# Six blocks of distance, eight transposed tiles, a bias on VectorE and another table of durations in a planned attention and Fourier kernel

## The chip, the core and the metric

One core of a Trainium2 chip runs the whole program. The engines are PE (TensorE, matrix products; PEld is its loading of weights), DVE (VectorE), ACT (ScalarE), POOL (GpSimd) and SP (SyncE, which only issues transfers here). The metric is the device time of one execution in microseconds (us); the time of a kernel is the median of its runs.

## The reference

Two layers read inputs of their own, and their outputs stand side by side, 2048 rows of 1024 + 1024 numbers.

```python
# A: attention with a window, 32 heads of 32 numbers
qkv = x @ wqkv                                   # 2048 x 3072
scores = q k^T * 32 ** -0.5
mask = (i - j >= 0) & (i - j < 256)              # a query sees itself and the 255 keys before it
p = softmax(where(mask, scores, -1e9))
a = (p v, heads side by side) @ wo               # 2048 x 1024
# B: Fourier mixing
y = dft_seq_re @ (x @ dft_hid_re.T) - dft_seq_im @ (x @ dft_hid_im.T)
concat([a, y], axis=-1)
```

All is in fp32 in the reference. The kernel holds each fp32 matrix as a sum of two fp16 matrices (hi and lo) and builds each large product out of three fp16 passes, hi.hi, hi.lo and lo.hi. The large square products are also cut in quarters and made from seven products instead of eight.

## The kernel before

**Stages.** First come the projections to q, k and v, which go to buffers in memory (`qs`, `vs`). Then attention runs block by block, and while it runs PE also does the second half of the projections and nearly the whole Fourier layer (lines with `m` at L720, 512 columns each). Last comes the product with `wo`. So PE has two streams of work, attention and the large products, and a number `rate` says how many attention blocks are recorded for each large product.

**One block of attention** (`s_step`) is 128 queries of two heads. There are 256 blocks, ordered by half of the sequence (`pr`), group of four heads (`g`), chunk of 512 tokens (`sc`), pair of heads (`hp`) and tile of 128 tokens (`i`). PE writes the scores against the last two key tiles into one of two PSUM banks `s`, and those against the third key tile into the bank `old` (L586). DVE joins them by a predicated copy (L597) and takes the row maximum `mx` (L602). POOL turns the maximum into the bias of the exponential (L609, `bias`, two numbers a row). ACT makes two exponentials (L612) and the hi half `hl` of the probabilities (L432), DVE the lo half (L436); only then is the `s` bank free. SP issues a transposing transfer from `hl` to `t` (L621), and POOL masks it: a masked copy `z` for the third tile (L627), and `t` itself (L630).

**The value products** (`v_step`) take two blocks at once: 24 small matmuls or fewer each (L662) into the one bank `pv`, then three DVE operations (L667, L669, L673) that divide and write the tile `o`. They are recorded `LAG` blocks behind the scores. After eight blocks `o_step` splits `o` in two halves `ohl`, transposes them to `ot` and stores that.

**What sets the order.** Nothing is issued as it is recorded. `Plan.op` records each operation with an engine, an assumed duration, and what it reads and writes. `Plan.close` gives it a due time, counted back from the PE operations in the order of their recording with their assumed durations summed. `Plan.run` then plays the program once with the assumed durations; each engine that comes free takes the operation with the earliest due time among those whose inputs are there. The order so found is fixed in each engine's queue; on the chip each engine works its queue strictly in order. So an assumed duration has no direct effect on the chip: it changes who stands before whom.

**Buffers.** A `Ring` of n buffers makes the (k+n)-th user wait for the last use of the k-th. In attention: `qk1` holds a chunk of keys (three transfers, L417, since hi stands twice), `qk0` one of queries, `vt` one of values; `hl`, `t`, `z` and `o` are as above. In the second half of the sequence (`pr` 1) each head group loads three key tiles in turn: half of chunk 1, chunk 2, chunk 3.

Of the kernel before, what the change touches and what calls it, by code (L numbers as in the profile page):

```python
# [10 lines left out]
F32 = mybir.dt.float32  # L11
# [33 lines left out]
LAG = 4  # L45
# [3 lines left out]
TBUF = 6  # L49
# [251 lines left out]
def c_act(n, ap=True):  # L301
    return 0.19 + 0.00084 * n + (0.09 if ap else 0.0)
# [26 lines left out]
def c_mm(n):  # L329
    return max(0.032, n / 2400.0 + 0.0025)  # L330
# [3 lines left out]
def fused_kernel(ctx: ExitStack, tc: tile.TileContext, xa, wqk, wv, wo, xb, wd, cs, out):  # L334
# [111 lines left out]
    def dve(cost, fn, r=(), w=(), port=False):  # L446
        op("DVE", cost, fn, r=r, w=w, port=port)
# [20 lines left out]
    def scale_of(key, v, s, wk, down=2.0 ** -14, loose=False):  # L468
        t1 = tops.pop(key)
        pt = old_ring.new()  # L470
        op("PE", 0.26, lambda: nc.tensor.transpose(pt.t[:, :P], t1.t[:, 0:1].to_broadcast([P, P]), ident),
# [8 lines left out]
        dve(0.53, rest, w=[wk])  # L480
# [44 lines left out]
    z_ring = att_ring("z", [P, 4, P], F16, 4)  # L525
    rs_ring = att_ring("rs", [P, 2, 2], F32, 2)
    o_ring = att_ring("o", [P, QB * P], F32, 3)

    def attention():
# [33 lines left out]
        def s_step(b):  # L563
# [8 lines left out]
            def scores(dst, k0, k_end, w):  # L572
                mats, cost, keys = [], 0.0, []
                for j in range(2):
                    h, k = 2 * hp + j, k0
                    while k < k_end:
# [4 lines left out]
                        cost += c_mm((k1 - k) * P) + 0.01  # L581
# [23 lines left out]
            if BIAS == "ACT":  # L605
                op("ACT", 0.387, lambda: nc.scalar.activation(bias.t, mx.t, AF.Identity, bias=pshift, scale=es),
                   r=[mx, "pshift", ("esc", g // 2)], w=[bias])
            else:
                op("POOL", 0.215, lambda: nc.gpsimd.tensor_scalar(bias.t, mx.t, es, PSHIFT, op0=ALU.mult, op1=ALU.add),  # L609
                   r=[mx, ("esc", g // 2)], w=[bias], port=True)  # L610
# [23 lines left out]
        def v_step(b):  # L634
# [3 lines left out]
            if (g, sc) not in cur:  # L638
                cur[g, sc] = o_ring.new()
            for r in (1, 0):  # L640
# [6 lines left out]
                for j in range(2):  # L647
                    at = (2 * hp + j) * VW
                    for m, (part, kb) in enumerate(seq):
# [4 lines left out]
                        cost += 0.034  # L654
# [10 lines left out]
                op("PE", cost, run, r=list(dict.fromkeys(keys)), w=[pv])  # L665
# [10 lines left out]
                rs.t.unsqueeze(3).to_broadcast([P, 2, 2, DH]), op=ALU.mult), r=[pv, rs], w=[(o, hp, i)])  # L676

        def o_step(g, sc):
            o = cur.pop((g, sc))
            keys = [(o, hp, i) for hp in range(2) for i in (0, 2)]  # L680
            ohl, ot = o_ring.new(), o_ring.new()
            half = lambda h: (lambda: ohl.t.bitcast(F16).rearrange("p (h c) -> p h c", h=2)[:, h])
            split(half(0), half(1), lambda: o.t, None, 512, keys, [(ohl, 0)], [(ohl, 1)])
            op("SP", C_TURN, lambda: nc.sync.dma_start_transpose(
                ot.t.bitcast(F16).rearrange("p (a q) -> p a q", q=P), ohl.t.bitcast(F16)),
               r=[(ohl, 0), (ohl, 1)], w=[ot], dma=turned(8))
            op("SP", C_ISSUE, lambda: nc.sync.dma_start(ots[sc, :, g].rearrange("c h t -> c (h t)"), ot.t.bitcast(F16)),
# [1007 lines left out]
```

## Time and profile before

| what | value |
|---|---|
| median of 3 runs | 1731.82 us (1731.67 to 1733.55) |
| the profiled execution | 1732.34 us, span 1730.6 us |
| PE busy | 1690.7 us, 98% |
| DVE busy | 1346.4 us, 78% |
| ACT busy | 1056.7 us, 61% |
| POOL busy | 776.7 us, 45% |
| clock granted to TensorE | 1.00 |

The span runs from the first to the last instruction of the profile. A group of the profile is named by line, engine, operation and tiles (out<-in). Behind its busy time stands the time in which the engine was idle just before it, and who ended that. Matmuls overlap: one of 512 columns is listed at 379 ns, though they follow each other faster than that.

### The profile page before, as it was taken

Reading aid. Unit: us, or ns where it says so; the run is one execution under the profiler, and the core shown is the slowest. Engines: PE = TensorE matmul, PEld = TensorE weight load, DVE = VectorE, ACT = ScalarE, POOL = GpSimd, SP = SyncE. Lnnn points to the kernel's source line nnn. Section 1 sums busy time; section 2 is a strip of 40 time slices with the busy share of each in tenths; the row PEclk is TensorE's granted clock in tenths of the full one; section 3 lists DMA queues with packets and bytes.
Section 4 is the critical chain, followed back from the end, with each engine's and each line's share of the span. In section 5 each row is a group of like instructions: output and inputs, shape, how many; then the busy total and the mean of one; then the engine's idle time right before and its main releaser. Section 6 shows DMA issues by size and latency. Waiting matters only on the chain.

```text
span 1730.6 us, 31866 instructions
## 1 busy us (share of the span) xinstructions
PE 1690.7 (98%) x11607; PEld 907.7 (52%) x11607; DVE 1346.4 (78%) x2294; ACT 1056.7 (61%) x1678; POOL 776.7 (45%) x979
## 2 busy tenths in 40 slices
PE   8999999999999999999999999999999999999998
PEld 3446787674545445545445555545555555544443
DVE  6978997677987888777798986789886688879641
ACT  7555635456767778777685756676665676553322
POOL 0133501314545646535765755676564666611000
PEclk9999999999999999999999999999999999999999
DMA  6389799999999779898499999769999658983331
GB/s 261 124 321 334 233 306 263 279 227 240 230 258 235 145 192 233 205 271 202 96 220 279 254 266 215 145 141 237 245 258 231 151 128 204 221 269 110 110 98 73
DMA packets 469918, 368.36 MB, mean 213 GB/s; under 512 B 341760, under 2 KB 412416, under 8 KB 469760
## 3 DMA queue, kind: packets, MB, share of 16 engines
q1 hardware_dynamic: 468896, 363.17, 81.0%
q0 software_dynamic: 864, 3.15, 1.2%
q8 instruction: 91, 1.49, 0.4%
q14 instruction: 67, 0.55, 0.1%
HBM read 195.97 MB, written 96.86 MB: 169 GB/s over the span
## 4 chain that ended last, share of the span: by engine, by line
PE 54%; DVE 15%; issue 8%; DMA 7%; ACT 7%; POOL 7%; SPq 1%; POOLq 0%; DVEq 0%; ACTq 0%
PE m L720 48%; PE pv L662 3%; POOL raw L1075 2%; DVE mx L602 2%; DVE st L1102 2%; ACT s L612 2%; POOL bias L609 2%; PE s L586 2%; DVE hl L436 2%; DMA t<-hl 1%; DVE s L597 1%; POOL t L630 1%; POOL z L627 1%; ACT hl L432 1%; DMA qk<-qs 1%
## 5 line engine op out<-in xcount | busy, mean ns | idle before, releaser
L720 PE MATMUL m<-reg,st 128*128 128x512 f16 x4776 | 1093.6, 379 | 13.6 <-DVE st L1102 3.6
L720 PEld LDWEIGHTS <-st 128*128 128x128 f16 x5400 | 512.5, 97 | 583.8 <-issue 15.1
L612 ACT ACTIVATE s<-s,bias,escs 128x256 f32<-128x256 f32 (+1 forms) x512 | 271.1, 530 | 286.2 <-POOL bias L609 277.4
L609 POOL TENSOR_SCALAR bias<-mx,escs 128x2 f32<-128x2 f32 x256 | 120.9, 472 | 400.5 <-DVE mx L602 308.6
L1075 POOL TENSOR_TENSOR raw<-raw,raw 128x512 f32<-128x512 f32 x128 | 175.8, 1374 | 186.6 <-DVE st L1102 174.7
L436 DVE TENSOR_TENSOR hl<-s,hl 128x512 f16<-128x512 f32 (+1 forms) x256 | 171.1, 669 | 96.5 <-ACT hl L432 95.7
L627 POOL TENSOR_SCALAR_AFFINE_SELECT z<-t 128x512 f16<-128x512 f16 x224 | 170.9, 766 | 60.0 <-DMA t<-hl 43.6
L630 POOL TENSOR_SCALAR_AFFINE_SELECT t<-t 128x512 f16<-128x512 f16 x224 | 170.5, 767 | 10.9
L602 DVE TENSOR_REDUCE mx<-s 128x2 f32<-128x512 f32 (+1 forms) x256 | 170.9, 668 | 4.8
L432 ACT ACTIVATE hl<-s 128x512 f16<-128x512 f32 (+1 forms) x256 | 148.0, 579 | 6.5 <-DMA t<-hl 3.1
L720 PEld LDWEIGHTS <-reg 128*128 128x128 f16 x1212 | 115.7, 98 | 63.2 <-issue 1.8
L1102 DVE SCALAR_TENSOR_TENSOR st<-raw,sc,st 128x1024 f16<-128x1024 f32 x96 | 134.1, 1400 | 16.5 <-ACT st L1101 16.2
L586 PEld LDWEIGHTS <-qk 96*128 96x128 f16 x1056 | 94.1, 97 | 85.8 <-issue 17.3
L1101 ACT ACTIVATE st<-raw,sc 128x1024 f16<-128x1024 f32 x96 | 109.6, 1146 | 34.5 <-PE m L720 14.5
L597 DVE COPY_PREDICATED s<-upper,old 128x256 f32<-128x256 uint32 x224 | 94.4, 421 | 29.3 <-PE old L586 21.8
L720 PE MATMUL m<-reg 128*128 128x512 f16 x480 | 114.7, 379 | 0.8 <-DVE reg L1512 0.5
L586 PE MATMUL s<-qk,qk 96*128 96x128 f16 (+1 forms) x608 | 96.0, 252 | 5.0 <-DVE hl L436 4.8
L720 PE MATMUL m<-xz,st 128*128 128x512 f16 x432 | 97.0, 379 | 3.4 <-ACT m L1193 3.4
L662 PE MATMUL pv<-vt,t 128*128 128x65 f16 x1984 | 98.4, 185 | 1.1 <-POOL t L630 1.0
L1512 DVE SCALAR_TENSOR_TENSOR ybig<-m,fu,ybig 128x512 f32<-128x512 f32 x112 | 83.4, 745 | 14.1 <-PE m L720 12.1
L662 PEld LDWEIGHTS <-t 128*128 128x128 f16 x1984 | 88.2, 96 | 9.8 <-POOL t L630 1.5
L662 PE MATMUL pv<-vt,z 128*128 128x65 f16 (+1 forms) x896 | 87.9, 185 | 4.2 <-DVE o L673 4.0
(172 smaller groups left out, 2124.7 us busy)
## 6 DMA issues: line engine op xcount, KB each, us to landing
raw<-in_cs_dram SPq DMA_DIRECT2D x64, 512.0 KB, 5.6
qk<-qs SPq DMA_DIRECT2D x192, 128.0 KB, 4.2
out_dram<-ybig SPq DMA_DIRECT2D x44, 512.0 KB, 5.4
qs<-ybig SPq DMA_DIRECT2D x64, 256.0 KB, 4.6
raw<-in_xb_dram SPq DMA_DIRECT2D x32, 512.0 KB, 5.4
raw<-in_wd_dram SPq DMA_DIRECT2D x32, 512.0 KB, 5.4
ybig<-out_dram SPq DMA_DIRECT2D x32, 512.0 KB, 5.3
vs<-ybig SPq DMA_DIRECT2D x32, 260.0 KB, 4.4
```

The costliest lines, as they stand in the source:

```text
L432: else nc.scalar.activation(dst(), src(), AF.Copy), r=r, w=w)
L436: op("DVE", c_dve(n), lambda: nc.vector.tensor_tensor(dst(), src(), hi(), op=ALU.subtract), r=r, w=w, port=port)
L586: nc.tensor.matmul(dst(j, a, e), qu.t[:, h, i * P:i * P + P], ku.t[:, h, ka:ke], start=True, stop=True, skip_group_check=True)
L602: dve(c_dve(2 * w), lambda: nc.vector.tensor_reduce(mx.t, sv(), axis=AX.X, op=ALU.max, negate=True), r=[(S, 0), (S, 1)], w=[mx])
L609: op("POOL", 0.215, lambda: nc.gpsimd.tensor_scalar(bias.t, mx.t, es, PSHIFT, op0=ALU.mult, op1=ALU.add), r=[mx, ("esc", g // 2)], w=[bias ...
L612: op("ACT", 0.32 + 0.00085 * w, lambda h=h: nc.scalar.activation(sv()[:, h], sv()[:, h], AF.Exp, bias=bias.t[:, h:h + 1], scale=es), r=[bi ...
L627: op("POOL", 0.637, lambda: nc.gpsimd.affine_select(out=z.t, in_=pk(), compare_op=ALU.is_gt, fill=0.0, base=0, pattern=[[0, 4], [-1, P]], ...
L630: op("POOL", 0.637, lambda: nc.gpsimd.affine_select(out=pk(), in_=pk(), compare_op=ALU.is_ge, fill=0.0, base=0, pattern=[[0, 4], [1, P]], ...
L662: nc.tensor.matmul(pvt()[:, r, j, lo:], lhs, vt.t[:, k % QB, at + lo:at + VW], start=a, stop=e, skip_group_check=True)
L720: nc.tensor.matmul(ps.t[:, j * n:j * n + n], lhs(), rhs(), start=first, stop=last, skip_group_check=True)
L1075: lambda: e.tensor_tensor(o(), a(), b(), op=ALU.subtract if sub else ALU.add), r=r, w=w, port=True)
L1102: op("DVE", c_dve(n, True), lambda: nc.vector.scalar_tensor_tensor(dst(1), src(), scl(), dst(0), op0=ALU.mult, op1=ALU.subtract), r=[*r, s ...
```

## The change

- `LAG` goes from 4 to 6: value products are recorded six blocks behind the scores.
- The ring `t` goes from 6 to 8 tiles. To make room, `qk1` goes from 3 to 2, `vt` from 3 to 2, `z` from 4 to 3, `o` from 3 to 1. The output halves `ohl` and `ot` now come from the rings `hl` and `t`, which the blocks of probabilities use. A key "turn" makes the first value product of a chunk follow the last `o` of the chunk before it.
- The bias moves from POOL to DVE (256 operations), with the assumed duration `C_TINY` (0.155).
- Assumed durations: ACT operations of 512 elements 0.60 where it was 0.62 (0.68 where 0.71, with a scale); a value matmul 0.0265 or 0.0297 where it was 0.034; a score matmul 0.01 less; a PE transposition 0.12 where it was 0.26; the three small operations of a scale 0.47 where it was 0.53.

```diff
-LAG = 4
+LAG = 6
...
-TBUF = 6
+TBUF = 8
...
 def c_act(n, ap=True):
-    return 0.19 + 0.00084 * n + (0.09 if ap else 0.0)
+    return 0.142 + 0.00089 * n + (0.083 if ap else 0.0)
...
-        op("PE", 0.26, lambda: nc.tensor.transpose(pt.t[:, :P], t1.t[:, 0:1].to_broadcast([P, P]), ident),
+        op("PE", 0.12, lambda: nc.tensor.transpose(pt.t[:, :P], t1.t[:, 0:1].to_broadcast([P, P]), ident),
...
-    k_ring = att_ring("qk1", [96, HG, CH], F16, 3)
+    k_ring = att_ring("qk1", [96, HG, CH], F16, 2)
...
-    vt_ring = att_ring("vt", [P, QB, HG * VW], F16, 3)
+    vt_ring = att_ring("vt", [P, QB, HG * VW], F16, 2)
...
-    z_ring = att_ring("z", [P, 4, P], F16, 4)
+    z_ring = att_ring("z", [P, 4, P], F16, 3)
...
-    o_ring = att_ring("o", [P, QB * P], F32, 3)
+    o_ring = att_ring("o", [P, QB * P], F32, 1)
...
-                        cost += c_mm((k1 - k) * P) + 0.01
+                        cost += c_mm((k1 - k) * P)
...
-            if BIAS == "ACT":
-                op("ACT", 0.387, lambda: nc.scalar.activation(bias.t, mx.t, AF.Identity, bias=pshift, scale=es),
-                   r=[mx, "pshift", ("esc", g // 2)], w=[bias])
-            else:
-                op("POOL", 0.215, lambda: nc.gpsimd.tensor_scalar(bias.t, mx.t, es, PSHIFT, op0=ALU.mult, op1=ALU.add),
-                   r=[mx, ("esc", g // 2)], w=[bias], port=True)
+            dve(C_TINY, lambda: nc.vector.tensor_scalar(bias.t, mx.t, es, PSHIFT, op0=ALU.mult, op1=ALU.add),
+                r=[mx, ("esc", g // 2)], w=[bias])
...
-                        cost += 0.034
+                        cost += 0.0265 if part else 0.0297
...
-                op("PE", cost, run, r=list(dict.fromkeys(keys)), w=[pv])
+                op("PE", cost, run, r=list(dict.fromkeys(keys)) + (["turn"] if begins else []), w=[pv])
...
-            ohl, ot = o_ring.new(), o_ring.new()
+            ohl, ot = hl_ring.new(), t_ring.new()
```

Every engine's queue is reordered by this, so three places are shown as they stand. First DVE, at the 33rd block (`s_32`; blocks are counted from 0, and `pv_14` serves blocks 28 and 29). Before:

```order
L597 COPY_PREDICATED s_32_4731<-upper_86,never_87 128x2x128
L597 COPY_PREDICATED s_33_4734<-upper_86,never_87 128x2x128
L602 TENSOR_REDUCE mx_32_4744<-s_32_4731 128x2
L602 TENSOR_REDUCE mx_33_4752<-s_33_4734 128x2
L436 TENSOR_TENSOR hl_32_4779<-s_32_4731,hl_32_4779 128x256
L667 RECIPROCAL rs_14_4801<-pv_14_4766 128x4
L669 TENSOR_REDUCE pv_14_4766<-pv_14_4766 128x128
L673 TENSOR_TENSOR o_9_4587<-pv_14_4766,rs_14_4801 128x2x64
L436 TENSOR_TENSOR hl_33_4805<-s_33_4734,hl_33_4805 128x512
```

and now:

```order
L597 COPY_PREDICATED s_32_4687<-upper_86,never_87 128x2x128
L602 TENSOR_REDUCE mx_32_4706<-s_32_4687 128x2
L605 TENSOR_SCALAR bias_32_4709<-mx_32_4706,escs_109 128x2
L436 TENSOR_TENSOR hl_35_4717<-s_32_4687,hl_35_4717 128x256
L597 COPY_PREDICATED s_33_4719<-upper_86,never_87 128x2x128
L664 RECIPROCAL rs_13_4757<-pv_13_4724 128x4
L602 TENSOR_REDUCE mx_33_4759<-s_33_4719 128x2
L666 TENSOR_REDUCE pv_13_4724<-pv_13_4724 128x128
L605 TENSOR_SCALAR bias_33_4771<-mx_33_4759,escs_109 128x2
L670 TENSOR_TENSOR o_3_4663<-pv_13_4724,rs_13_4757 128x2x64
```

The bias now stands in the DVE queue behind its maximum, for block 32 at once, for block 33 with one operation of another kind between them; of the 256, 41 follow at once, 188 with one operation between and 27 with two to five. The value products served here are one pair further behind.

Second POOL at the same blocks, before, where the two biases stand ahead of the masks of blocks 30 and 31 (in the new order no bias row is left on POOL):

```order
L609 TENSOR_SCALAR bias_32_4755<-mx_32_4744,escs_109 128x2
L609 TENSOR_SCALAR bias_33_4757<-mx_33_4752,escs_109 128x2
L627 AFFINE_SELECT z_22_4799<-t_30_4709 128x512
L630 AFFINE_SELECT t_30_4709<-t_30_4709 128x4x128
L627 AFFINE_SELECT z_23_4827<-t_31_4728 128x512
L630 AFFINE_SELECT t_31_4728<-t_31_4728 128x4x128
L609 TENSOR_SCALAR bias_34_4893<-mx_34_4886,escs_109 128x2
```

Third SP, where the second half of the sequence begins and the keys of chunk 2 (`qk1_17`) are loaded. Before, ring of three:

```order
L621 DMA_TRANSPOSE t_123_10567<-hl_123_10533 128x8x128 [waits DMAHW1_49,DVE_49,PE_49]
L417 DMA qk1_17_10592<-qs_57 32x4x512 [waits DMAHW2_49,PE_49]
L417 DMA qk1_17_10592<-qs_57 32x4x512 [waits DMAHW3_49]
L417 DMA qk1_17_10592<-qs_57 32x4x512 [waits DMAHW4_49]
L684 DMA_TRANSPOSE o_44_10605<-o_43_10540 128x8x128 [waits DMAHW5_49,DVE_49]
L417 DMA raw_134_10621<-in_wd_dram 128x1024 [waits DMAHW6_49,DVE_49]
```

and now, ring of two:

```order
L617 DMA_TRANSPOSE t_138_10549<-hl_138_10534 128x8x128 [waits DMAHW2_49,DVE_49]
L617 DMA_TRANSPOSE t_139_10600<-hl_139_10581 128x8x128 [waits DMAHW3_49,DVE_49]
L417 DMA qk1_17_10616<-qs_57 32x4x512 [waits DMAHW4_49,PE_49]
L417 DMA qk1_17_10616<-qs_57 32x4x512 [waits DMAHW5_49]
L417 DMA qk1_17_10616<-qs_57 32x4x512 [waits DMAHW6_49]
L417 DMA ybig_83<-out_0_dram 128x1024 [waits DMAHW7_49,DVE_49,Activation_49]
```

The first of the three transfers waits for PE in both. Before, the buffer it fills is that of `qk1_14`, whose last score matmul stands 19.9 us of PE work ahead of the first that reads `qk1_17` (matmuls counted in the PE queue, each at the pace of the trace, given in the prediction). Now it is that of `qk1_15`, whose last score matmuls (blocks 127 and `old_124`) stand 28 matmuls of 512 columns, 24 value matmuls and 2 of 128 columns ahead, 6.8 us.

More of the change, by code (lines that the diff above doesn't have):

```diff
@@ L478, in rest @@
             nc.vector.reciprocal(s, v)
-        dve(0.53, rest, w=[wk])
+        dve(0.47, rest, w=[wk])
     vx = const.tile([P, 2, 2], F32, name="vx")
```

15 lines of the change are left out of this document (8 added, 7 removed).

## The prediction, on record before the result was known

> **What bounds the kernel now.** I read the page's first part, then the busy times by stage, then who PE waits for, then one wait back to its cause.
>
> ```profile
> span 1730.6 us, 31866 instructions
> PE 1690.7 (98%) x11607; PEld 907.7 (52%) x11607; DVE 1346.4 (78%) x2294; ACT 1056.7 (61%) x1678; POOL 776.7 (45%) x979
> ```
>
> PE is the bound: it is idle for 1730.6 - 1690.7 = 39.9 us. The change adds and removes no PE instruction, so only waits can go or come. The busy times in three stretches (before, during and after attention; columns: start and end, length, then PE, PEld, DVE, ACT, POOL) say where the idle time lies:
>
> ```profile
> 0.00:262.00 262.00, 253.17 (x1527) 152.87 (x1528) 218.94 (x284) 149.44 (x197) 62.48 (x69) 1.00 0.75 262
> 262.00:1515.00 1253.00, 1230.42 (x9128) 661.69 (x9127) 999.08 (x1869) 834.81 (x1393) 700.00 (x901) 1.00 0.91 217
> 1515.00:1731.00 216.00, 207.12 (x956) 93.12 (x954) 128.37 (x143) 72.43 (x88) 14.23 (x10) 1.00 0.42 131
> ```
>
> 8.8 us before attention, 1253.0 - 1230.4 = 22.6 us during it, 8.5 us after it. PE's waits in the middle stretch (us in total, times, longest):
>
> ```profile
> PE s L586 <- DVE hl L436: 4.8, 8, 1.3
> PE pv L662 <- DVE o L673: 4.0, 6, 1.4
> PE m L720 <- DVE st L1102: 3.4, 4, 1.0
> PE old L586 <- DVE sc L1060: 2.4, 4, 1.1
> PE old L586 <- DVE s L597: 2.2, 1, 2.2
> PE m L720 <- ACT m L1193: 1.5, 2, 1.0
> PE pv L662 <- POOL t L630: 1.0, 2, 0.7
> ...
> PE m L720 <- DVE ybig L1512: 0.6, 2, 0.3
> ```
>
> These are 34 short waits in all (21.4 us with the four rows left out), and DVE ends most of them. DVE is busy 999 of 1253 us: no bound, but its queue is where something stands in front of what PE needs. The chain and the timeline of one such wait:
>
> ```profile
> 431.94 4.10 PE m L720 x19
> 436.04 0.22 PE s L586 x2
> 436.26 0.11 PE old L586 x2
> 436.37 0.67 PE pv L662 x24
> ```
>
> ```profile
> 433.81 1.15 POOL L609 TENSOR_SCALAR bias<-mx,escs 128x2 f32<-128x2 f32 x1 [8.65 <-DVE mx L602]
> 434.99 1.11 ACT L612 ACTIVATE s<-s,bias,escs 128x256 f32<-128x256 f32 x2 [2.75 <-POOL bias L609]
> 437.55 0.59 ACT L1193 ACTIVATE m<-m 128x512 f32<-128x512 f32 x1
> 438.19 1.02 PE L720 MATMUL m<-reg,st 128*128 128x512 f16 x4 [1.03 <-ACT m L1193]
> ```
>
> A bias of two numbers a row took 1.15 us on POOL; ACT stood 2.75 us for it, so its copy of a product's bank began at 437.55, and PE stood 1.03 us for the copy. The chain also gives PE's true pace: 4.10 / 19 = 0.216 us for 512 columns. Such a matmul is listed at 379 ns (the page's group of L720), so each wait of PE hides another 0.16 us: 34 waits cost 22.6 + 34 x 0.163 = 28.1 us. I sum in shown idle time and multiply by 28.1 / 22.6 = 1.24 at the end.
>
> **The change part by part.**
>
> *The bias leaves POOL.*
>
> ```profile
> L609 POOL TENSOR_SCALAR bias<-mx,escs x256: 259/268/1813, 264.1 to 1500.1; 128x2 f32<-128x2 f32 x128
> ...
>   POOL bias L609: 277.4, 183
> ```
>
> ```profile
> L609 POOL TENSOR_SCALAR bias<-mx,escs 128x2 f32<-128x2 f32 x256 | 120.9, 472 | 400.5 <-DVE mx L602 308.6
> L1065 DVE TENSOR_SCALAR sc<-sc 128x1 f32<-128x1 f32 x32 | 4.9, 154 | 1.1
> L602 DVE TENSOR_REDUCE mx<-s 128x2 f32<-128x512 f32 (+1 forms) x256 | 170.9, 668 | 4.8
> ```
>
> Half the biases take 268 ns, the mean is 472 and the longest 1813; ACT waits 277.4 us for them, 183 times. On DVE the nearest row, a tiny operation with the same opcode, takes 154 ns. But 215 of the 256 now have another operation between maximum and bias, which costs up to one maximum (0.67 us); so the exponential starts hardly earlier on average, only more evenly. What PE can get is in the waits at the end of that chain: 4.8 (bank `s`, freed by `hl`) + 1.5 (copies on ACT) = 6.3. Bounds -6.3 and 0; I take -2, nearer to nothing because of those 215.
>
> *DVE gets it:* 256 x 0.154 = 39.4 us, DVE in the stretch from 999.1 to 1038.5, its idle time from 253.9 to 214.5. DVE ends 17.6 us of PE's waits (the rows above with DVE, and 0.2 in a row left out). If waits grow as its work, +0.7; if as one over its idle time, 17.6 x 253.9 / 214.5 - 17.6 = +3.2. I take +2, the middle.
>
> By the Trainium skill (Advanced Engine Details and Errata, Mode Summary) GpSimd shares VectorE's second SBUF port and the two block each other, so every instruction that leaves POOL also gives DVE time back; the spread from 259 to 1813 ns agrees on POOL's side, and no row shows what DVE lost. By that rule this term would be its lower bound of 0.7, and the sum 1.6 us lower.
>
> *Six blocks of distance, eight `t`.* They serve the wait of value products for masks, 1.0 us; the other wait of `pv`, 4.0 us, is for its single bank, which stays. POOL loses 120.9 us of work ahead of its masks. Against it, `z` has three tiles and `o` one: DVE's write of a new `o` must wait until the old one is split, and `pv` is held meanwhile; one more wait of the longest kind seen there is 1.4 us. Bounds -1.0 and +1.4; I take -0.5.
>
> *Two key and value tiles.* In the second half each head group loads three key tiles, so chunk 2 now takes the buffer of the scores just before it, eight times. In the new PE queue the work between last and next use is 6.0, 6.9, 6.9 and 7.7 us at the four tightest of these (9 to 14 at the others), and 4.7 and 6.7 at two value tiles.
>
> ```profile
> L586 PE MATMUL s<-qk,qk x608: 216/270/275, 262.4 to 1492.1; 96*128 96x256 f16 x88, 96*128 96x128 f16 x64
> L586 PE MATMUL old<-qk,qk x448: 216/218/222, 262.8 to 1492.3; 96*128 96x128 f16 x150
> L417 SPq DMA_DIRECT2D qk<-qs x216: 302/431/2507, 250.7 to 1417.6; - x108
> ...
> DMA to landing us min/median/max: 1.8/4.2/8.8
> ```
>
> ```profile
> L417 SPq DMA_DIRECT2D vt<-vs x40: 360/436/1606, 256.5 to 1451.7; - x40
> ...
> DMA to landing us min/median/max: 2.3/4.6/8.0
> ```
>
> Three issues and the last landing are 3 x 0.431 + 4.2 = 5.5 us, for values 0.436 + 4.6 = 5.0. At the median only the value tile with 4.7 is late, by 0.3. With the longest landings (10.1 and 8.4) the six are short by 4.1, 3.2, 3.2, 2.4, 3.7 and 1.7, 18 together. Bounds 0 and 9 (half of them at their longest); I take +2.
>
> The Trainium skill (DMA: Bandwidth & Descriptors, the table of cost components) gives a transfer some 2.0 us plus its bytes over 436 per ns, 2.3 us for 128 KB; the median here is 4.2 and only the shortest is below it, so the trace differs. By the rule no reload would be late and the sum would be 2.5 us lower.
>
> *The table of durations.* It touches only who stands before whom. What does the old table get wrong? The 24 value matmuls of the chain take 0.67 us, 0.0279 each; the table said 0.034 and now says 0.0281 on average. Two score matmuls take 0.22, two of `old` 0.11; the table had 0.01 more each.
>
> ```profile
> L662 PE MATMUL pv<-vt,t 128*128 128x65 f16 x1984 | 98.4, 185 | 1.1 <-POOL t L630 1.0
> L662 PE MATMUL pv<-vt,z 128*128 128x65 f16 (+1 forms) x896 | 87.9, 185 | 4.2 <-DVE o L673 4.0
> ```
>
> (1984 + 896) x 0.0061 + (608 + 448) x 0.01 = 17.6 + 10.6 = 28 us: the old plan believed PE 2.3% slower in this stretch than it is. So PE comes to each wait earlier than planned, and a queue that was just in time is late. The bias was also planned at 0.215, under half its mean. With both mended, orders should fit better. How much is that worth? Below, nothing, since every other queue is shuffled too. Above, the best quarter of attention is the mark:
>
> ```profile
> 1000.00:1250.00 250.00, 243.20 (x1886) 128.69 (x1885) 202.28 (x389) 165.47 (x277) 162.11 (x207) 1.00 0.90 208
> 1250.00:1500.00 250.00, 248.41 (x1841) 129.64 (x1840) 198.85 (x376) 160.16 (x264) 154.10 (x196) 1.00 0.86 198
> ```
>
> PE idles 6.8 us in one and 1.6 in the next, with DVE and POOL as busy in both; so waits hang on the order, not on load. At 1.6 per 250 us the stretch would idle 8.0, and 14.6 us would be gone with all terms. 12 of it can fall to this one; I take half, -6.
>
> The stretches before and after attention are reordered too (their PE work is the same); nothing in the table aims at them, so 0.
>
> *Sum:* -2 + 2 - 0.5 + 2 - 6 = -4.5 us, times 1.24 = -5.6. The profiled execution took 1732.3 us, 0.5 above the median; so 1726.7 for it, and 1726 for the median. All gains at their bounds: -14.6 x 1.24 = -18, 1713.7. All losses and no gain: (3.2 + 1.4 + 9) x 1.24 = +17, 1749.
>
> **Rivals.**
>
> *Larger gain, 1714.* The order becomes as good as in the best quarter, everywhere. For it: load is no obstacle there. Against it: it leaves no room for new waits.
>
> *No change, 1731.* Old waits go and as many come, since each queue is shuffled and the plan still knows nothing of long landings. For it: 34 small waits in twelve groups, not one cause. This is also the case where the change does not do what its table promises.
>
> *Slower through reloads, 1739.* PE waits at the six tight places, 2.5 us each (landings near 8 us): +15. The other terms are -6.5 x 1.24 = -8. For it: the transfers are busy 0.91 of the stretch. Against it: the median landing fits five of six places. It outweighs the gains from 1.4 us per place, and is told from no change from 1.9.
>
> *Slower through DVE, 1739.* The biases stand in front of the operations that free PE's banks, and a quarter of the 39.4 us reaches PE: +10, with the hidden part +12. Of the table's gain half stays (-4 with the hidden part), the first and third term give -3, reloads +2.5; together +7.5. For it: DVE ends 17.6 of 21.4 us of waits. Against it: it idles 214 us even then. What decides is whether the bias stands before `hl`, `st` and `o` when PE is about to need them; it outweighs those gains from a tenth of the 39.4 us.
>
> **How the numbers follow.** Forecast 0.38, larger gain 0.15, no change 0.22, reloads 0.14, DVE 0.11. About 0.2% (3.5 us) is what a measurement of this kernel can tell from none. Faster 0.38 + 0.15 = 0.53, same 0.22, slower 0.25. The range must reach both sides: 1713 to 1740, down to all gains and up to the two slower cases; the forecast's own is 1721 to 1730.
>
> **What would show it.** PE busy stays near 1691 and its idle time in the attention stretch falls from 22.6 to about 18. POOL falls by 121 us, DVE grows by about 40 (by 50 if the bias takes 0.2). ACT's wait for the bias, 277 us, shrinks and is now for DVE. PE's waits for a transfer into `qk` or `vt` come to about 2 us; above 8 the reload rival is right. If PE's waits for DVE grow beyond 17.6 us, DVE is the cause. I am wrong if PE's idle time in that stretch stays or grows.

## The result: slower by 0.8%

The changed kernel takes 1744.59 us (median of 6 runs, 1740.72 to 1750.54), the kernel before 1731.7 in the same comparison (1730.02 to 1733.55). The ratio is 1.0082 with a 95% interval of [1.0068, 1.0096], so 13 us were lost where 5.6 were forecast as gained. The time lies above the range as well.

### The profile page after: what moved, and what is told of

Its sections match the earlier page's. It is cut to its first block, busy times and chain, and to the rows that moved or that the text cites. A ratio compares the mean times of both kernels' runs of the same rounds, so it can differ in the third digit from the quotient of the medians.

```text
span 1748.8 us, 31763 instructions
## 1 busy us (share of the span) xinstructions
PE 1696.6 (97%) x11607; PEld 908.8 (52%) x11607; DVE 1416.6 (81%) x2550; ACT 1053.7 (60%) x1678; POOL 657.8 (38%) x723
## 4 chain that ended last, share of the span: by engine, by line
PE 66%; DVE 15%; ACT 9%; issue 5%; DMA 4%; POOL 1%; SPq 0%; ACTq 0%; DVEq 0%; POOLq 0%
PE m L717 59%; ACT s L608 3%; PE pv L659 3%; DVE hl L436 3%; DVE mx L602 2%; PE s L586 2%; DVE bias L605 2%; ACT hl L432 2%; DVE st L1099 2%; DMA t<-hl 1%; DVE s L597 1%; ACT st L1098 1%; PE old L586 1%; ACT reg L432 1%; DVE reg L436 1%
## 5 line engine op out<-in xcount | busy, mean ns | idle before, releaser
L1099 DVE SCALAR_TENSOR_TENSOR st<-raw,sc,st 128x1024 f16<-128x1024 f32 x96 | 128.2, 1337 | 12.8 <-ACT st L1098 11.9
L586 PE MATMUL s<-qk,qk 96*128 96x128 f16 (+1 forms) x608 | 95.9, 253 | 22.1 <-DVE hl L436 21.2
L605 DVE TENSOR_SCALAR bias<-mx,escs 128x2 f32<-128x2 f32 x256 | 94.2, 368 | 1.4
```

The lines of the kernel that those rows point to most:

```text
L586: nc.tensor.matmul(dst(j, a, e), qu.t[:, h, i * P:i * P + P], ku.t[:, h, ka:ke], start=True, stop=True, skip_group_check=True)
L605: dve(C_TINY, lambda: nc.vector.tensor_scalar(bias.t, mx.t, es, PSHIFT, op0=ALU.mult, op1=ALU.add), r=[mx, ("esc", g // 2)], w=[bias])
L1099: op("DVE", c_dve(n, True), lambda: nc.vector.scalar_tensor_tensor(dst(1), src(), scl(), dst(0), op0=ALU.mult, op1=ALU.subtract), r=[*r, s ...
```

## The profile after

The profiled execution of the changed kernel took 1750.54 us, 6 us above its median. First the head of its page, then its busy times in the three stretches of the prediction (start and end, length, then PE, PEld, DVE, ACT, POOL with their instructions, the granted clock, the busy share of the transfers, GB/s):

```profile
span 1748.8 us, 31763 instructions
PE 1696.6 (97%) x11607; PEld 908.8 (52%) x11607; DVE 1416.6 (81%) x2550; ACT 1053.7 (60%) x1678; POOL 657.8 (38%) x723
```

```profile
0.00:262.00 262.00, 254.29 (x1545) 154.11 (x1546) 222.83 (x288) 149.57 (x197) 62.01 (x69) 1.00 0.75 264
262.00:1515.00 1253.00, 1217.50 (x8964) 652.31 (x8963) 1053.95 (x2092) 826.22 (x1386) 570.21 (x635) 1.00 0.91 213
1515.00:1749.00 234.00, 224.80 (x1102) 102.39 (x1099) 139.80 (x173) 77.87 (x96) 25.63 (x20) 1.00 0.46 137
```

The loss is in the attention stretch. PE idles 1253.0 - 1217.5 = 35.5 us there instead of 22.6, and gets through 8964 matmuls instead of 9128; the other stretches idle 7.7 and 9.2 us, nearly as before. POOL lost 119 us of work. DVE gained 70, where 40 were forecast. The waits of PE in that stretch (us in total, times, longest):

```profile
PE s L586 <- DVE hl L436: 21.2, 23, 6.3
PE m L717 <- ACT m L1190: 3.5, 5, 0.9
PE m L717 <- DVE st L1099: 3.4, 6, 1.2
PE pv L659 <- DVE o L670: 2.0, 2, 1.6
PE old L586 <- DVE s L597: 1.7, 4, 0.8
...
PE s L586 <- DMA qk<-qs: 0.2, 1, 0.2
```

One row grew by more than 2 us: PE's wait for a free score bank, which comes free when DVE has made the lo half `hl`. It was 4.8 us. One of its 23 waits, of 6.3 us, goes back to a late transfer (last section); the other 22 come to 14.9 us. The waits for a reload of keys, the rival at 1739, are 0.2 us. Now the moved operation: its durations (min/median/max ns), its group row, and who waits for it:

```profile
L605 DVE TENSOR_SCALAR bias<-mx,escs x256: 212/228/1416, 262.5 to 1514.2; 128x2 f32<-128x2 f32 x128
...
L605 DVE TENSOR_SCALAR bias<-mx,escs 128x2 f32<-128x2 f32 x256 | 94.2, 368 | 1.4
```

```profile
  ACT s L608: 235.8, 148
```

The mean is 368 ns, not the 154 of the prediction, and the longest is 1416. It looks as it did on POOL (472 in the mean, 1813 at most). One of the long ones in the timeline, with what ran on POOL (start, length):

```profile
573.86 1.70 POOL L1072 TENSOR_TENSOR raw<-raw,raw 128x512 f32<-128x512 f32 x1
...
574.35 1.23 DVE L605 TENSOR_SCALAR bias<-mx,escs 128x2 f32<-128x2 f32 x1
575.50 0.48 DVE L597 COPY_PREDICATED_SCALAR s<-upper,never 128x256 f32 x1
575.52 1.27 POOL L1072 TENSOR_TENSOR ybig<-ybig 128x512 f32<-128x512 f32 x1
575.62 1.11 ACT L608 ACTIVATE s<-s,bias,escs 128x256 f32<-128x256 f32 x2 [0.98 <-DVE bias L605]
```

POOL's operation ends at 573.86 + 1.70 = 575.56, the bias at 574.35 + 1.23 = 575.58. The same holds all over the trace. Of the 256 biases, 135 meet no POOL operation and take 212 to 230 ns; 121 overlap with one, with a median of 472 ns. The 80 of these that take over 300 ns end 22 to 37 ns after a POOL operation has ended. So an operation of two numbers a row stands in DVE's queue until POOL is done with what it is doing, and everything behind it in that queue stands as well: here ACT's exponentials 0.98 us, elsewhere the copies and lo halves that free PE's banks.

## Experiments

Theories, with the letters under which some expectations name them. A: the bias on DVE is the cause (B and C, in the first four: the table, the rings). A1: its price is the wait for POOL, in whatever order; A2: its price is the order that a plan made which was told 0.155. N: any new order moves the time this much. L: DVE simply has too much work. M: what the plan counts for the bias is not what it takes. P: the two-column operation waits for POOL's running operation, and the plan, which holds 0.155 us for it, knows nothing of that. A last question is how far the plan's wrong number matters by itself.

Each result is a median with its ratio to the kernel before and a 95% interval. Where two experiments are compared, both ratios are to that kernel.

### One part alone, and all but one

The table of durations alone, all its numbers in the kernel before:

```diff
...
-                        cost += 0.034
+                        cost += 0.0265 if part else 0.0297
...
```

> The kernel before with the new table of durations and nothing else. Theory A (the 256 biases on DVE, at 0.37 us each instead of the 0.154 I assumed, delay what frees the score banks): the table is harmless, 1726 to 1733. Theory B (the new table makes a worse order): 1740 to 1746, PE's waits for hl in the score banks near 20 us as in the change. Theory C (rings and distance): 1726 to 1733.

1734.17 us, 1.0022 [1.0009, 1.0035], 1 us above what was expected. Alone it gains nothing.

The bias alone:

```diff
-                op("POOL", 0.215, lambda: nc.gpsimd.tensor_scalar(bias.t, mx.t, es, PSHIFT, op0=ALU.mult, op1=ALU.add),
-                   r=[mx, ("esc", g // 2)], w=[bias], port=True)
+            dve(C_TINY, lambda: nc.vector.tensor_scalar(bias.t, mx.t, es, PSHIFT, op0=ALU.mult, op1=ALU.add),
+                r=[mx, ("esc", g // 2)], w=[bias])
```

> The kernel before with only the bias moved from POOL to DVE. Theory A: 1740 to 1746, DVE busy grows by 70 us, PE's waits for hl in the score banks grow from 4.8 to about 20 us. Theory B and theory C: within 4 us of 1731.7.

1742.5 us, 1.0070 [1.0048, 1.0093], as theory A expected, but PE's wait for `hl` grew to 8.1 us, not to the 20 expected; PE idles 30.8 us in that stretch, over more and shorter waits. Its biases, and the first row of PE's waits in the attention stretch:

```profile
L605 DVE TENSOR_SCALAR bias<-mx,escs x256: 193/228/1992, 263.9 to 1507.5; 128x2 f32<-128x2 f32 x128
...
PE s L586 <- DVE hl L436: 8.1, 15, 1.9
```

Six blocks of distance and the rings alone (`LAG`, `TBUF`, the four smaller rings, halves in `hl` and `t`, the key "turn"):

```diff
-LAG = 4
+LAG = 6
...
-TBUF = 6
+TBUF = 8
...
```

> The kernel before with only the distance of six blocks, eight t tiles, the smaller rings and the output halves in the rings hl and t. Theory C (the smaller and shared rings hold back hl, t and z, and with them the score banks): 1738 to 1746, with waits of ACT for the transfer of t out of hl. Theory A and theory B: 1729 to 1734.

1727.98 us, 0.9977 [0.9965, 0.9989], 1 us below what theories A and B expected, and far from C's 1738.

The changed kernel with only the bias put back on POOL, planned there as before:

```diff
-            dve(C_TINY, lambda: nc.vector.tensor_scalar(bias.t, mx.t, es, PSHIFT, op0=ALU.mult, op1=ALU.add),
-                r=[mx, ("esc", g // 2)], w=[bias])
+                op("POOL", 0.215, lambda: nc.gpsimd.tensor_scalar(bias.t, mx.t, es, PSHIFT, op0=ALU.mult, op1=ALU.add),
+                   r=[mx, ("esc", g // 2)], w=[bias], port=True)
```

> The change with the bias back on POOL, everything else as changed. Theory A: back to the time before or below it, 1722 to 1732, PE's waits for hl in the score banks back near 5 us. Theory B and theory C: 1740 to 1746, those waits still near 20 us.

1723.17 us, 0.9955 [0.9939, 0.9972]. Its attention stretch:

```profile
262.00:1515.00 1253.00, 1240.77 (x9184) 667.40 (x9181) 1015.24 (x1879) 833.15 (x1399) 712.40 (x904) 1.00 0.92 218
```

PE idles 12.2 us there. All parts but the bias gain 8 us, and the bias costs 1.0082 / 0.9955 = 1.013, 22 us. Theory A holds by both tests: put in alone it loses 12 us, taken out it gives back more than the whole loss.

How much does any new order move? One number that plans small DVE operations, shifted by 0.005 us in each kernel, gives a new order and nothing else:

```diff
-C_TINY = 0.155
+C_TINY = 0.150
```

> The kernel before with one assumed duration of tiny DVE operations at 0.150 instead of 0.155: another order, nothing else. Theory N (any new order scatters by as much as the change cost): 8 us or more away from 1729. Theory L (DVE's load with the bias) and theory M (a mismatch between what the plan counts for the bias and what it takes): within 4 us of 1729.

The same in the changed kernel, with 0.160:

> The change with the same duration (here that of the bias too) at 0.160 instead of 0.155: another order. Theory N: 8 us or more away from 1744. Theory L and theory M: 1739 to 1749.

The two took 1733.9 us, 1.0026 [1.0012, 1.0039], and 1744.83 us, 1.0088 [1.0070, 1.0106]. The second is where the changed kernel was, the first 3 to 4 us above where the kernel before was. N falls for the loss of 13 us, as far as one new order of each can show; but some 4 us can be luck of an order, and the results of the table alone and of the rings alone are no larger.

The second also shows what of the profile after belongs to one execution. Its profiled execution took 1744.76 us, near the median:

```profile
262.00:1515.00 1253.00, 1224.79 (x9031) 656.92 (x9031) 1062.17 (x2105) 830.70 (x1392) 569.93 (x637) 1.00 0.91 214
```

PE idles 28.2 us there, not 35.5, and waits 9.2 us for `hl`, not 21.2. Its waits for DVE are 21.2 us in all, against 17.6 before, and its busy time in the whole kernel is 1697.0 us, against 1690.7. So which row grows depends on the order; in both, PE's waits and its busy time grow together.

### Load, or waits for POOL

The bias on ACT, planned there at 0.32:

```diff
-            dve(C_TINY, lambda: nc.vector.tensor_scalar(bias.t, mx.t, es, PSHIFT, op0=ALU.mult, op1=ALU.add),
+            op("ACT", 0.32, lambda: nc.scalar.activation(bias.t, mx.t, AF.Identity, bias=pshift, scale=es),
...
```

> The change with the bias on ACT (an Identity with scale and bias, planned at 0.32), replanned. Theory A1: DVE is free of it and no operation waits for POOL's port: 1718 to 1728. Theory A2: a third order, anywhere from 1720 to 1745.

1719.97 us, 0.9946 [0.9926, 0.9967]. A bias takes 384 ns there in the mean, longer than on DVE in the changed kernel, but always the same:

```profile
L605 ACT ACTIVATE bias<-mx,pshift,escs x256: 372/387/398, 263.5 to 1481.4; 128x2 f32<-128x2 f32 x128
```

This takes DVE's work away too, so it does not separate L from P. The next does. The order of the changed kernel is kept, the same on every engine, and each bias is issued as two operations of one column:

```diff
+            def two():
+                for h in range(2):
+                    nc.vector.tensor_scalar(bias.t[:, h:h + 1], mx.t[:, h:h + 1], es, PSHIFT, op0=ALU.mult, op1=ALU.add)
+
-            dve(C_TINY, lambda: nc.vector.tensor_scalar(bias.t, mx.t, es, PSHIFT, op0=ALU.mult, op1=ALU.add),
+            dve(C_TINY, two,
```

> The change's plan as it is, but each bias as two DVE operations on one column each. Theory P (a DVE operation on two columns stands until a POOL operation under way has ended, one on a single column doesn't, and these waits are the price): each near 0.2 us with no long ones, 1732 to 1739. Theory L: the pair takes as long as the one took on average, 1740 to 1750.

1724.18 us, 0.9960 [0.9945, 0.9974]. The engines, the biases, the attention stretch and PE's first wait there:

```profile
PE 1693.2 (98%) x11607; PEld 909.2 (53%) x11607; DVE 1412.0 (82%) x2806; ACT 1054.1 (61%) x1678; POOL 667.3 (39%) x723
...
L607 DVE TENSOR_SCALAR bias<-mx,escs x512: 193/203/215, 265.9 to 1495.2; 128x1 f32<-128x1 f32 x171
...
262.00:1515.00 1253.00, 1234.90 (x9144) 664.62 (x9142) 1064.70 (x2380) 833.86 (x1395) 591.97 (x646) 1.00 0.92 217
...
PE s L586 <- DVE hl L436: 8.1, 11, 3.2
```

DVE is as busy as in the changed kernel (1412 against 1417 us), with 256 operations more. The two of a pair overlap: from the start of the first to the end of the second they take 326 ns in the mean, a ninth less than the 368 of the wide one, and all biases together 83 us of DVE where they took 94. But none takes over 215 ns, although POOL works as before beside them. PE's idle time falls from 35.5 to 18.1 us and the kernel is 1.2% faster (0.9960 / 1.0082), 20 us, and lies below the 1732 to 1739 that was expected. L falls: it expected 1740 to 1750, and 11 us less work, on an engine that idles over 180 us of the stretch, is too little for 20 us. P holds: that a third of the biases stood, for up to 1.4 us, was the price in this order. (This profiled execution took 1731.65 us, 7 above its median; its longest wait, 3.2 us, is part of that.)

### The same order, another engine

Is it the order, or what the bias meets in it? Each of the two orders is kept as its plan made it, and only the engine that the bias is issued on is swapped: first the changed kernel with the bias on POOL, then the kernel before with it on DVE.

```diff
-            dve(C_TINY, lambda: nc.vector.tensor_scalar(bias.t, mx.t, es, PSHIFT, op0=ALU.mult, op1=ALU.add),
+            dve(C_TINY, lambda: nc.gpsimd.tensor_scalar(bias.t, mx.t, es, PSHIFT, op0=ALU.mult, op1=ALU.add),
```

> The change's plan as it is (the planner still counts the bias as a DVE operation of 0.155), but each bias is issued on POOL at its place in the common order; DVE's queue is that of the change without the 256 biases. Theory A1 (the price is physical: the bias on DVE takes 0.37 us because it stands until a POOL operation under way has ended, whatever the order): 1723 to 1732. Theory A2 (the price is the order: the planner, told 0.155, lined the queues up badly): 1738 or more.

```diff
-                op("POOL", 0.215, lambda: nc.gpsimd.tensor_scalar(bias.t, mx.t, es, PSHIFT, op0=ALU.mult, op1=ALU.add),
+                op("POOL", 0.215, lambda: nc.vector.tensor_scalar(bias.t, mx.t, es, PSHIFT, op0=ALU.mult, op1=ALU.add),
```

> The plan of the kernel before as it is (the planner still counts the bias as a POOL operation of 0.215), but each bias is issued on DVE at its place in the common order. Theory A1: 1740 to 1746, the bias near 0.37 us on DVE, its long ones ending with a POOL operation. Theory A2: 1728 to 1735.

The two took 1744.96 us, 1.0095 [1.0080, 1.0110], and 1776.46 us, 1.0278 [1.0263, 1.0294]. The first is what A2 expected, against A1; the second lies 30 us and more above what either expected. On POOL in the changed order the bias takes 262 to 2278 ns (448 in the mean), and PE's wait for `hl` is 17.1 us. So DVE free of the bias (1353 us busy) does not help as long as the bias still varies like that. Then each order again without any wait between DVE and POOL in the bias: the first with it on ACT, the second with two single columns on DVE (`two()` as above).

```diff
-            dve(C_TINY, lambda: nc.vector.tensor_scalar(bias.t, mx.t, es, PSHIFT, op0=ALU.mult, op1=ALU.add),
+            dve(C_TINY, lambda: nc.scalar.activation(bias.t, mx.t, AF.Identity, bias=pshift, scale=es),
```

> The order of the changed kernel, row for row, with each bias issued on ScalarE instead of VectorE; the plan still holds 0.155 us for it, on VectorE. A bias takes 372 to 398 ns on ScalarE (measured in the run with the bias planned there) and never stands for GpSimd. Theory of the wait for GpSimd's running operation: the time falls to 1724 to 1732, although ScalarE gets 256 x 0.39 = 100 us that no plan knows of; PE's waits for hl below 9 us. Theory that this order itself is bad for any bias that takes longer than planned: 1738 to 1748, as with the bias on GpSimd in this order (1745), with PE waiting over 15 us for hl or the copies of ScalarE.

```diff
-                op("POOL", 0.215, lambda: nc.gpsimd.tensor_scalar(bias.t, mx.t, es, PSHIFT, op0=ALU.mult, op1=ALU.add),
+            op("POOL", 0.215, two,
```

> The order of the kernel before, row for row, with each bias issued as two single-column operations on VectorE; the plan still holds them on GpSimd. VectorE gets the same 84 to 94 us as in the run with the two-column bias there (1776). Theory of the wait for GpSimd's running operation: without it most of the loss is gone, 1733 to 1748. Theory that VectorE work which the plan doesn't hold is the cost: 1765 to 1780, with PE's waits for hl near 20 us.

The two took 1730.9 us, 0.9998 [0.9984, 1.0012], and 1750.02 us, 1.0122 [1.0104, 1.0141]. The first is 14 us below the changed kernel, as the theory of the wait expected, with 256 x 0.38 = 98 us on ACT that its plan does not hold; the expectation of 9 us for PE's wait for `hl` was missed (11.3). The second is 26 us below its twin, a little above what was expected; 20 us stay lost. Its biases take 216 ns at most, so these are not waits of a bias for POOL; what is left, by elimination, is 83 us of DVE work that the plan had put on POOL. It shows where PE waits for DVE:

```profile
PE s L586 <- DVE hl L436: 14.5, 20, 6.2
PE pv L662 <- DVE o L673: 4.4, 8, 0.8
```

So there are two prices, the wait for POOL and time that the plan does not hold, and neither order is bad by itself.

### What the plan knows

The planner has a rule for the shared resource, and the operations that use it carry a flag:

```python
            if o.port:
                other = "POOL" if e == "DVE" else "DVE"
                cost += max(0.0, lock[other] - t)
                lock[e] = t + cost
```

The bias on POOL carried `port=True`; `dve` sets it to `False` unless told, and the changed bias is recorded so. First the flag and the undisturbed duration, then no flag but the whole mean:

```diff
-            dve(C_TINY, lambda: nc.vector.tensor_scalar(bias.t, mx.t, es, PSHIFT, op0=ALU.mult, op1=ALU.add),
-                r=[mx, ("esc", g // 2)], w=[bias])
+            dve(0.225, lambda: nc.vector.tensor_scalar(bias.t, mx.t, es, PSHIFT, op0=ALU.mult, op1=ALU.add),
+                r=[mx, ("esc", g // 2)], w=[bias], port=True)
```

> The change with the bias still on DVE, but the planner told what the trace shows: 0.225 us and a port shared with POOL, so that it waits in the plan for a POOL operation under way. Theory A1: 1734 to 1744, since the work stays on DVE. Theory A2: 1721 to 1728, as good as with the bias on POOL.

```diff
-            dve(C_TINY, lambda: nc.vector.tensor_scalar(bias.t, mx.t, es, PSHIFT, op0=ALU.mult, op1=ALU.add),
+            dve(0.38, lambda: nc.vector.tensor_scalar(bias.t, mx.t, es, PSHIFT, op0=ALU.mult, op1=ALU.add),
```

> The change with the bias on DVE, planned at 0.38, the mean it takes there. Theory M: 1720 to 1733, since the plan now counts the 55 us of DVE work that it left out. Theory L: 1738 to 1748, PE's waits for DVE as before this edit.

The two took 1745.09 us, 1.0103 [1.0083, 1.0123], and 1729.05 us, 0.9986 [0.9973, 0.9999]. The first lies just above what A1 expected, far from A2's; the second is in M's range. The flag did nothing for the time: in that run 137 biases overlap with a POOL operation, and 91 of them take over 300 ns (121 and 80 without it). The mean gave 16 us back, with the biases as long as ever. Their rows, first with the flag, then with 0.38 and with PE's first wait there:

```profile
L605 DVE TENSOR_SCALAR bias<-mx,escs x256: 209/228/1323, 265.2 to 1504.9; 128x2 f32<-128x2 f32 x128
```

```profile
L605 DVE TENSOR_SCALAR bias<-mx,escs x256: 209/228/1310, 263.1 to 1486.1; 128x2 f32<-128x2 f32 x128
...
PE s L586 <- DVE hl L436: 4.9, 8, 1.8
```

The flag adds time only where the plan itself sees the two engines meet; the mean adds it to every bias. Whether that is why the one is 16 us worse than the other was not tried, and stays open.

Single columns in the changed kernel, planned near their true time, bring both remedies together (against the run with single columns above):

```diff
-            dve(C_TINY, two,
+            dve(0.36, two,
```

> The changed kernel with two single-column operations for the bias, planned at 0.36 us on VectorE instead of 0.155. Theory of the wait for GpSimd's running operation: the price is gone already, so the true duration in the plan adds only the noise of a new order, 1719 to 1727 (1724.2 without it). Theory that what counts is a plan with enough time in it: clearly faster than 1724, 1712 to 1718.

1712.02 us, 0.9899 [0.9884, 0.9914]: 12 us less than with 0.155 in the plan, and 33 less than the changed kernel. The expectation of 1719 to 1727 was wrong; time that the plan does not hold is a cost of its own, as far as one new order can show (12 us is three times what the new orders above moved). Its head, its attention stretch and PE's waits there:

```profile
span 1708.0 us, 32275 instructions
PE 1683.5 (99%) x11607; PEld 908.9 (53%) x11607; DVE 1404.6 (82%) x2806; ACT 1049.9 (61%) x1678; POOL 665.0 (39%) x723
...
262.00:1515.00 1253.00, 1243.93 (x9222) 672.06 (x9220) 1067.79 (x2396) 837.94 (x1403) 595.45 (x650) 1.00 0.93 221
...
PE m L720 <- ACT m L1193: 3.0, 3, 1.7
PE m L720 <- DVE st L1102: 1.3, 1, 1.3
...
PE s L586 <- DVE hl L436: 0.8, 3, 0.4
```

PE idles 9.1 us, and the wait for `hl` is gone.

### Wider rings, and the move alone

The bias on ACT, planned at 0.387, with rings of four tiles `hl` and `z`; and the single columns at 0.36 with the same rings:

```diff
-    hl_ring = att_ring("hl", [P, 8 * P], F16, 3)
+    hl_ring = att_ring("hl", [P, 8 * P], F16, 4)
...
-    z_ring = att_ring("z", [P, 4, P], F16, 3)
+    z_ring = att_ring("z", [P, 4, P], F16, 4)
```

> The changed kernel with the bias on ScalarE, planned there at 0.387 us, and rings of four tiles hl and z instead of three. With three tiles it was 1720.0. Theory: no port wait, and room for a late transfer or a late mask; 1714 to 1720. If the rings were no limit: 1718 to 1723, the same within the noise of a new order.

> The changed kernel with two single-column operations for the bias on VectorE, planned at 0.36 us, and rings of four tiles hl and z instead of three. With three tiles it was 1712.0. PE idles 9 us in the attention stretch there, with 0.8 us for hl. Theory that the rings still limit: 1704 to 1709. Theory that nothing is left to take there: 1709 to 1715, the noise of a new order.

1711.27 us, 0.9894 [0.9877, 0.9910], and 1718.06, 0.9925 [0.9906, 0.9944]. With ACT 9 us less than at three tiles (and 0.32), with DVE 6 more. Both missed what was expected, the first below it, the second above. The rings are no clear limit, and again a new order is worth several us either way. The two best, 1712.0 and 1711.3, cannot be told apart; both beat the kernel before by 1%.

Last, the kernel before with nothing but the bias as two single columns on DVE at 0.36:

```diff
-                op("POOL", 0.215, lambda: nc.gpsimd.tensor_scalar(bias.t, mx.t, es, PSHIFT, op0=ALU.mult, op1=ALU.add),
-                   r=[mx, ("esc", g // 2)], w=[bias], port=True)
+            dve(0.36, two, r=[mx, ("esc", g // 2)], w=[bias])
```

> The kernel before with one edit: the bias as two single-column operations on VectorE, planned there at 0.36 us. Theory that the move of the bias gains by itself when its form and its plan are right (as from 1723.2 to 1712.0 with the other parts): 1717 to 1724. Theory that it gains only with six blocks of distance and the new durations: 1726 to 1735.

1738.73 us, 1.0051 [1.0032, 1.0070], slower, where both expectations were below. Where? The attention stretch in three pieces, this kernel first, then the kernel before:

```profile
262.00:880.00 618.00, 615.28 (x4532) 341.19 (x4531) 520.58 (x1158) 429.97 (x731) 250.02 (x277) 1.00 0.91 222
880.00:1000.00 120.00, 104.95 (x716) 52.18 (x715) 98.50 (x214) 68.55 (x109) 51.98 (x57) 0.93 0.98 230
1000.00:1515.00 515.00, 512.20 (x3806) 268.31 (x3804) 440.16 (x997) 334.10 (x555) 279.13 (x305) 1.00 0.89 204
```

```profile
262.00:880.00 618.00, 606.50 (x4475) 335.56 (x4474) 479.19 (x890) 425.11 (x720) 294.93 (x396) 1.00 0.91 220
880.00:1000.00 120.00, 118.05 (x823) 60.54 (x822) 110.34 (x199) 80.75 (x130) 80.43 (x93) 1.00 1.04 255
1000.00:1515.00 515.00, 505.88 (x3833) 265.59 (x3832) 409.54 (x782) 328.94 (x545) 324.65 (x412) 1.00 0.88 204
```

In 1133 of 1253 us PE idles 5.5 us, where the kernel before idles 20.6: there the move gains by itself. In the 120 us between, it idles 15.1 instead of 2.0, at a granted clock of 0.93. All four runs of this kernel show a lower granted clock over the whole execution, 0.993 to 0.996 where the kernel before has 0.999 to 1.0, so the piece is not the bad luck of the one profiled. At its start four transfers land late, after 12.5 to 14.4 us (issues of 870 to 900 us, two of the four shown: KB if any, us to landing), and behind one of them ACT and then PE stand:

```profile
raw<-in_cs_dram SPq DMA_DIRECT2D x1, 512.0 KB, 14.4
...
o<-o SPq DMA_TRANSPOSE x1, 14.1
```

```profile
894.75 1.06 ACT L1000 ACTIVATE junk<-raw 128x1024 uint8<-128x1024 f32 x1 [6.78 <-DMA raw<-in_cs_dram]
...
899.48 0.59 PE L586 MATMUL s<-qk,qk 96*128 96x256 f16 x2 [6.20 <-DVE topone L464]
```

That these transfers are the cause of the whole piece is likely by their place, but no run here took them away.

## Why the prediction was wrong

The step that failed is **"DVE gets it: 256 x 0.154"**, taken at +2 with bounds of 0.7 and 3.2. Measured, the bias on DVE costs 22 us (changed kernel against the same with the bias on POOL). That holds the term of POOL's relief too, so it stands against -2 + 2 = 0. In PE's idle time of the attention stretch it is 35.5 against 12.2 us, or 28.2 against 12.2 with the ordinary execution of the reshuffled kernel. Three things were wrong in the step.

*The row.* The 154 ns were those of an operation of one column with an immediate. The nearest row by shape was another, and three more show what it would meet (all of the kernel before; min/median/max ns):

```profile
L978 DVE TENSOR_SCALAR escs<-vxc,scw,topone x4: 289/290/551, 103.8 to 198.4; 128x4 f32<-128x4 f32 x4
L436 DVE TENSOR_TENSOR hl<-s,hl x256: 409/684/693, 266.1 to 1503.4; 128x512 f16<-128x512 f32 x112, 128x256 f16<-128x256 f32 x16
L436 DVE TENSOR_TENSOR o<-o,o x32: 674/693/1483, 315.5 to 1517.9; 128x512 f16<-128x512 f32 x32
L1102 DVE SCALAR_TENSOR_TENSOR st<-raw,sc,st x96: 1270/1284/3581, 574.2 to 1569.7; 128x1024 f16<-128x1024 f32 x96
```

Operations of DVE whose inputs all lie in SBUF (`o`, `st`) sometimes take twice their median or more; `hl`, which reads the PSUM bank `s`, never does. The slow ones are slow for POOL: the seven `o` over 860 ns all end 540 to 547 ns after a POOL operation has ended, the fourteen `st` over 1600 ns 1073 to 1087 ns after one, so most of their work begins when POOL is done. The prediction says that "no row shows what DVE lost"; these rows did, and the bias, from `mx` to `bias`, is of the first kind.

*The sign of a rule.* The prediction took from the Trainium skill (Advanced Engine Details and Errata, Mode Summary) only that POOL and DVE block each other, and let DVE gain by it. The same table names what a VectorE mode with two read ports asks for: source and destination in SBUF, and the outermost dimension that is not one even in both (or odd and equal). Two columns meet that; one column has no such dimension. The runs agree: in the same order 1416 ns at most for two columns, 215 for one. By that page, then, the moved operation carries its wait along to DVE.

*The measure.* Load was made the measure ("if waits grow as its work"). DVE as busy, with operations that do not wait, is 20 us faster, so load was not it. The plan held the same wrong price: told 0.38 instead of 0.155, with the biases as long as before, the kernel took 1729.05 us. The wait and the plan that does not hold it are one fault with two remedies; either gives back 16 to 20 us, both together 33. The rival "slower through DVE" named the right place, biases in front of what frees PE's banks, but it too priced the 39.4 us of work.

The other terms, point by point:

- *The bias leaves POOL, -2.* ACT's wait for it went from 277 to 236 us, as the forecast said it would shrink, and PE got nothing of that. In a form that does not wait, the move is worth some 10 us (0.9955 to 0.9899), of which some may be luck of the order.
- *Two key and value tiles, +2.* PE waits 0.2 us for keys and nothing for values. Landings were no shorter than before (8.7 us at most for keys, 10.8 for values), but PE did not wait for the longest. The rival of reloads falls. With it falls the largest part of the prediction's sum of all losses, which at 1749 does reach above the measured time.
- *Six blocks and eight `t`, -0.5,* and with them the reloads: some 3 us gained alone (0.9977), about as much as a new order can give.
- *The table, -6.* Alone it gave nothing (1.0022); with the rings, 8 us together (0.9955), where these three terms had -4.5 x 1.24 = -5.6. That sum was near; how it splits between them is not settled.
- *The test that was named* was right: PE's waits for DVE were to tell DVE as the cause if they grew beyond 17.6 us, and they came to 29.1 (the four rows above with DVE, and two of 0.4 that are left out there), or 21.2 in the reshuffled kernel. PE's busy time is 1696.6 us instead of 1691, which has a reason of its own, told last.

## What to carry to other kernels

When an operation moves to another engine, take its price from a row with the same operands in the same memories and the same shape, and look at the longest of that row, not at the median: a spread there is a wait that moves along. In a queue that is fixed in advance, it also counts whether the plan holds the operation's time. In the changed kernel the tiny operation on DVE between two SBUF tiles, beside a busy POOL, was better split into single columns (20 us) or given to ACT (24 us). That is no rule for every order: in the kernel before, single columns on DVE were 9 us slower than the bias on POOL.

## What the runs showed of the hardware

**A DVE operation of two columns, from SBUF to SBUF, waits for POOL's running operation, one of a single column does not** (212 to 1416 ns in the changed kernel, 193 to 215 in the same order), by the rows above. The wait can go on through more than one. In the reshuffled changed kernel the longest bias stood through five POOL operations that overlapped one another, and ended 32 ns after the fifth:

```profile
L605 DVE TENSOR_SCALAR bias<-mx,escs x256: 195/223/4525, 264.7 to 1509.4; 128x2 f32<-128x2 f32 x128
```

**After a wait of several us PE runs at half pace for a while.** In the profiled execution of the changed kernel a transposing transfer landed 14.5 us after its issue (10.1 at most in the kernel before); the ring of three `hl` tiles made ACT stand for it, then DVE, then PE:

```profile
1459.18 1.89 PE L717 MATMUL m<-reg,st 128*128 128x512 f16 x8
...
1466.05 0.60 ACT L432 ACTIVATE hl<-s 128x512 f16<-128x512 f32 x1 [7.86 <-DMA t<-hl]
1466.68 0.69 DVE L436 TENSOR_TENSOR hl<-s,hl 128x512 f16<-128x512 f32 x1 [6.58 <-ACT hl L432]
...
1467.42 0.58 PE L586 MATMUL s<-qk,qk 96*128 96x256 f16 x2 [6.35 <-DVE hl L436]
...
1467.80 3.62 PE L717 MATMUL m<-reg,st 128*128 128x512 f16 x8
```

The granted clock was 0.50 in what follows (its columns as above):

```profile
1467.40:1472.00 4.60, 4.58 (x14) 1.93 (x14) 3.39 (x5) 1.44 (x2) 4.32 (x4) 0.50 1.14 277
```

Eight matmuls took 1.89 us before the wait and 3.62 after it. So a wait of 6.35 us costs 1.7 us more at once, and appears as more busy time of PE, not as idle time; the 1696.6 us are partly this. By the Trainium skill (TensorE: Matmul & The Clock Gate, Part 1) the clock is halved after an idle window of about 3.4 us until PE has been busy as long; the rows agree with that, 6.35 us idle and then 4.6 us at 0.50. The other runs agree on the long waits: each of the six of 4.08 to 6.87 us was followed by a granted clock of 0.50 for 3.4 or 6.8 us. But a long wait is not the only way there. In the changed kernel 20 matmuls took 6.16 us from 854.05 on, where 20 had taken 4.48 just before, after two waits of 1.76 and 1.55 us.
